# First feed forward block of an attention and feed forward kernel: order of steps from a list scheduler in place of a table

## The chip, the core and the metric

The kernel runs on one core of a Trainium2 chip. A core has TensorE (PE in the profile; its loads of the stationary operand are PEld), VectorE (DVE), ScalarE (ACT), GpSimd (POOL) and SyncE (SP, which issues DMAs). Each engine takes its instructions from a queue of its own, in program order, and waits at semaphores for what others produce. The metric is device time in microseconds. Three runs of the kernel before took 734.34, 735.73 and 742.5 us; the median is 735.73.

## What is computed

Attention with a learned bias over relative positions, then two feed forward blocks. Only the first of these is touched:

```python
def _moe_ref(x, w_in, w_out, a, b):      # x 1152 x 512, d_ff 2048
    h = x @ w_in
    h2 = h * h
    h3 = h2 * h
    P = a[0] + a[1] * h + a[2] * h2 + a[3] * h3
    Q = 1.0 + np.abs(b[0]) * np.abs(h) + np.abs(b[1]) * h2
    g = P / (Q + 1e-06)
    return (g @ w_out).astype(np.float32)
```

The second block is `maximum(0.01 * h, h)` between two products of the same sizes.

## The kernel before

Matrices are split in a high and a low part of a short float type, and a product is the sum of three: high by high, high by low, low by high.

The hidden width of 2048 is cut into NF = 16 slices of 128, called f. For each f there is a round of steps:

- `gemm1(f, kk)`, kk = 0 to 3 (PE, line 399): 9 matmuls each, 36 for one f, into one of two PSUM areas `ph`. An f can only start when `r_v(f - 2)` has read the area.
- the rational function, on tiles of 128 x 1152: `r_abs` (ACT, 435), `r_s1` (ACT, 439), `r_qa` (DVE, 443), `r_qq` (ACT, 446), `r_h2` (DVE, 449), `r_h3` (DVE, 452), `r_ln` (ACT, 456), `r_exp` (ACT, 459), `r_q1` (ACT, 464), `r_e` (POOL, 470; on DVE, 468, for f = 0, 1, 2, and then without `r_q1`), `r_v` (DVE, 473), `r_fin` (DVE, 476). `r_e` needs `r_exp` and `r_q1`; `r_v` needs `r_h3` and `r_exp`; `r_fin` needs `r_e` and `r_v`. Tiles rotate through 3 buffers (`s`, `qq`), 2 (`r`) and 1 (`ah`).
- `split_hi` (ACT, 489) and `split_lo` (POOL, 494; on DVE for f = 0, 1, 9) make the two parts `gh` and `gl` of the result. Both need `r_fin`.
- the weights for later f, a group t at a time: `w_load` (SP, 337), three `w_dve` steps that turn 64-bit floats into 32-bit (DVE, 356, 358, 360; operands `biasr` and `raw`, all in SBUF), `w_hi` (ACT, 370) and `w_lo` (POOL, 378). A group has two weight slices, the last ones have one and their steps are half as wide. `w_dve` of a group writes the one buffer `raw` that `w_lo` of the group before reads.

The second product runs over blocks of f (`BLOCKS = [1, 2, 2, 2, 3, 3, 3]`). For each block it makes 12 tiles of 128 x 384 (`g2_feat`; PE, line 976, 3 matmuls for each f of the block), and each tile is added to a sum in SBUF by DVE (line 984, 0.55 us; for the first block ACT copies it, 982). Tiles rotate through two PSUM buffers `py`.

What sets the order before is the table `PLAN1`: a list of (step, name) pairs. A loop counts s up, four s for one f, and at each s emits the instructions of the table in its order, each for the f that (s - step)/4 gives. Tiles of the second product are put in between by a credit that grows at an even rate; a block comes into the queue `G2_LAG[0]` = 12 steps after its last f. For the last f, all steps go in thirds of the columns. So each f repeats the same order on each engine:

```python
PLAN1 = [
    (4, "r_v"),
    (5, "w_lo", 0),
    (-3, "gemm1", 0),
```

`START` is a list of steps that are emitted ahead of the loop (the last steps of f = 0, `gemm1` of f = 1, four tiles of the first block); it stays. The second feed forward block has its own table, `PLAN2`, and follows.

Of the kernel before, what the change touches and what calls it, by code (L numbers as in the profile page):

```python
# [31 lines left out]
PLAN1 = [
    (4, "r_v"),
    (5, "w_lo", 0),
    (-3, "gemm1", 0),
    (-3, "gemm1", 1),
    (2, "r_h3"),
    (8, "split_hi"),
    (-2, "gemm1", 2),
    (2, "w_dve", 0),  # L40
    (3, "w_dve", 2),
    (-2, "gemm1", 3),
    (0, "r_qa"),
    (5, "w_hi", 1),
    (8, "split_lo", (1, 9)),
    (-1, "r_abs"),
    (0, "r_s1"),
    (3, "r_exp"),
    (5, "w_lo", 1),
    (1, "r_h2"),  # L50
    (4, "r_q1"),
    (1, "r_qq"),
    (2, "w_dve", 1),
    (4, "w_hi", 0),
    (2, "r_ln"),
    (7, "r_fin"),
    (4, "w_load"),
    (4, "r_e"),
]
# [211 lines left out]
def attn_bias_moe_kernel(  # L271
# [754 lines left out]
    w_ops = {x.__name__: x for x in (w_dve, w_hi, w_lo)}
    w_ops["w_load"] = lambda t: w_load(t + 1)
    for m, plan, g2_lag, fn, args in (
        ("1", PLAN1, G2_LAG[0], g2_feat, [(n, c) for n in range(KD) for c in range(3)]),
        ("2", PLAN2, G2_LAG[1], g2_tok, [(t,) for t in range(NT // 128)]),  # L1030
    ):
# [17 lines left out]
        for s in range(4 * (NF + 5)):
            ready = s - g2_lag  # L1050
            if m == "1" and (s == G2_FIRST or ready == 0):
                if s == G2_FIRST:
                    queue += [(0, a) for a in first]
                    rate = len(args) / 4
            elif ready % 4 == 0 and ready // 4 in block_end:
# [93 lines left out]
```

## Time and profile before

| | |
|---|---|
| runs | 734.34, 735.73, 742.5 us |
| profiled execution | 741.0 us, of which the span from first to last instruction 739.2 us |
| granted TensorE clock, mean of the span | 0.937 |
| PE, DVE, ACT, POOL busy | 615.1, 527.4, 391.7, 365.0 us |
| first feed forward block | about 273 to 535 us of the span |

A busy share is an average over the whole span; the stages differ. In the slices of the page PE is busy to 60 to 90% from 270 to 510 us, and to 100% behind that. Where an engine waits, the profile names what ended the wait.

### The profile page before, as it was taken

The page shows a single profiled execution, that of the slowest core. Times are in us where ns is not written, and L with a number is a line of the kernel's source. Part 1 is how long each engine was busy: PE and PEld are TensorE (multiplying, and loading weights), DVE is VectorE, ACT ScalarE, POOL GpSimd, SP SyncE. Part 2 cuts the span into 40 slices and gives each one's busy share as a digit, 9 for nine tenths or more (in the row PEclk, how much of TensorE's full clock was granted, in tenths as well). Part 3 has the DMA queues.
Part 4 walks back from the last instruction along what each step waited for, and adds up shares of the span by engine and source line. Part 5 has one row for each costly group of instructions (what it writes and reads, how often), then busy time and mean ns, then how long its engine had stood idle before and what let it go on. Part 6 is the DMA issues. An engine that isn't in the chain of part 4 may idle for free. (4 is left out here: it accounts for less than half of the span.)

```text
span 739.2 us, 11793 instructions
## 1 busy us (share of the span) xinstructions
PE 615.1 (83%) x4595; PEld 542.0 (73%) x4595; DVE 527.4 (71%) x837; ACT 391.7 (53%) x590; POOL 365.0 (49%) x270
## 2 busy tenths in 40 slices
PE   4566669988887867669797778977999999999998
PEld 2333458777776866668686778976999989999876
DVE  7999688888788488867577787675725664654463
ACT  5687367787686448664555556662325423323220
POOL 4676567787688212263544435545125535345240
PEclk9998789999899889779999899999999999999999
DMA  3999989999999611211111121001113313222013
GB/s 126 142 134 133 155 169 197 195 200 189 179 207 177 162 66 55 107 57 58 57 58 58 57 108 35 30 29 57 58 58 114 113 58 114 75 96 86 29 57 129
DMA packets 104359, 77.35 MB, mean 105 GB/s; under 512 B 86512, under 2 KB 86896, under 8 KB 104304
## 3 DMA queue, kind: packets, MB, share of 16 engines
q1 hardware_dynamic: 100704, 68.97, 41.3%
q10 hardware_dynamic: 3600, 7.64, 3.9%
q8 instruction: 36, 0.59, 0.4%
q14 instruction: 19, 0.16, 0.1%
HBM read 42.38 MB, written 2.36 MB: 61 GB/s over the span
## 5 line engine op out<-in xcount | busy, mean ns | idle before, releaser
L399 PE MATMUL ph<-bias,bias 128*128 128x384 f32 x1152 | 227.3, 353 | 24.2 <-DVE s L473 21.1
L399 PEld LDWEIGHTS ph<-bias,bias 128*128 128x128 f32 x1152 | 216.4, 201 | 31.5 <-issue 23.6
L824 POOL TENSOR_TENSOR hl<-ex,hl 128x512 f16<-128x512 f32 (+2 forms) x105 | 104.3, 1011 | 36.5 <-DVE hl L811 19.9
L494 POOL TENSOR_TENSOR gl<-s,gh 128x1152 fp32r<-128x1152 f32 (+1 forms) x31 | 77.8, 2513 | 89.0 <-ACT gh L489 89.0
L976 PE MATMUL py<-gh,wo 128*128 128x384 f32 x288 | 85.5, 355 | 27.6 <-DVE bias L984 27.6
L759 PE MATMUL ps<-kt,qz 128*128 128x288 f32 x432 | 84.0, 336 | 19.5 <-DVE mn L771 9.9
L759 PEld LDWEIGHTS ps<-kt,qz 128*128 128x128 f32 x432 | 67.1, 210 | 32.0 <-DVE mn L771 14.6
L378 POOL TENSOR_TENSOR bias<-raw,bias 128x512 fp32r<-128x512 f32 x37 | 48.5, 1314 | 73.2 <-ACT bias L370 66.9
L976 PEld LDWEIGHTS py<-gh,wo 128*128 128x128 f32 x288 | 55.4, 197 | 31.9 <-DVE bias L984 31.9
L1017 DVE TENSOR_TENSOR bias<-pz,bias 128x512 f32<-128x512 f32 x48 | 33.1, 689 | 60.0 <-PE pz L1009 59.8
L1009 PE MATMUL pz<-wo,gh 128*128 128x512 f32 (+1 forms) x240 | 74.4, 386 | 0.3 <-DVE bias L1017 0.3
L378 POOL TENSOR_TENSOR wo<-raw,wo 128x512 fp32r<-128x512 f32 x23 | 29.8, 1294 | 78.5 <-ACT wo L370 78.5
L685 POOL TENSOR_TENSOR t<-t,te 128x576 f32<-128x576 f32 x36 | 50.8, 1415 | 33.1 <-ACT t L681 15.1
L670 PEld LDWEIGHTS <-coef 128*32 128x32 f16 x1152 | 27.7, 104 | 52.6 <-issue 40.6
L787 ACT ACTIVATE ex<-pt,mn 128x576 f32<-128x576 f32 x72 | 55.3, 767 | 18.1 <-DVE mn L771 10.9
L489 ACT ACTIVATE gh<-s 128x1152 fp32r<-128x1152 f32 (+1 forms) x33 | 36.1, 1100 | 48.9 <-DVE s L476 41.2
L984 DVE TENSOR_TENSOR bias<-py,bias 128x384 f32<-128x384 f32 x72 | 39.0, 553 | 31.4 <-PE py L976 31.3
L356 DVE TENSOR_SCALAR raw<-biasr 128x1024 int32<-128x1024 int32 (+1 forms) x40 | 28.5, 712 | 40.5 <-POOL bias L378 19.2
L976 PE MATMUL py<-gl,wo 128*128 128x384 f32 x156 | 54.2, 347 | 0.0
L771 DVE CUSTOM_DVE_ANT_0 pt<-ps,bias 128x576 f32<-128x576 f32 x64 | 47.7, 747 | 7.6 <-PE ps L759 5.2
L1009 PEld LDWEIGHTS pz<-wo,gh 128*128 128x128 f32 x240 | 44.3, 188 | 8.1 <-DVE bias L1017 0.7
L1009 PE MATMUL pz<-wo,gl 128*128 128x512 f32 (+1 forms) x129 | 50.1, 389 | 0.0
(134 smaller groups left out, 1131.9 us busy)
## 6 DMA issues: line engine op xcount, KB each, us to landing
biasr<-in_moe_w_in SPq DMA_DIRECT2D x32, 512.0 KB, 4.3
biasr<-in_moe_w_out SPq DMA_DIRECT2D x32, 512.0 KB, 3.3
bias<-bb SPq DMA_DIRECT2D x32, 288.0 KB, 8.8
vl<-in_v ACTq DMA_DIRECT2D x8, 320.0 KB, 3.6
ql<-in_q ACTq DMA_DIRECT2D x8, 288.0 KB, 4.3
kl<-in_k ACTq DMA_DIRECT2D x8, 288.0 KB, 4.9
out<-bias SPq DMA_DIRECT2D x8, 256.0 KB, 2.0
biasr<-bb SPq DMA_DIRECT2D x8, 144.0 KB, 8.9
```

The lines of the kernel that those rows point to most:

```text
L378: G.tensor_tensor(lo_, raw[:, x], hi_.bitcast(F32), ALU.subtract)
L399: PE.matmul(ps[:, c, 0:CH], w[:, sl], x[kk][:, c * CH:(c + 1) * CH], start=(kk == 0 and n == 0), stop=(kk == KD - 1 and n == 2),)
L489: A.activation(part(gts[f][0], c), part(s1[f], c), AF.Copy)
L494: eng.tensor_tensor(part(gl, c), part(s1[f], c), part(gh, c).bitcast(F32), ALU.subtract)
L685: G.tensor_tensor(t1, t0, te[:, S - 16 * n:2 * S - 16 * n], ALU.mult)
L759: PE.matmul(ps[:, c, 0:288], lt[:, a], kts[i][:, b, 288 * c:288 * c + 288], start=(n == 0), stop=(n == 2),)
L771: V.tensor_tensor_reduce(out=c2(pt), in0=s_ps.pop((i, j))[:, :, 0:288], in1=c2(bsrc), op0=ALU.add, op1=ALU.min, scale=1.0, scalar=3.0e38, ...
L787: A.activation(et, pt, AF.Exp, bias=mn, scale=-1.0, accum_out=sums[i][:, col:col + 1],)
L824: engines[j in at].tensor_tensor(hl[:, xs, dst], e9[:, xs, src], hl[:, xs, src], ALU.subtract)
L976: PE.matmul(ps[:, 0:CH], w[:, sl], gts[f][x][:, cs], start=(f == f0 and m == 0), stop=(f == f0 + nf - 1 and m == 2),)
L984: V.tensor_tensor(dst, ps[:, 0:CH], dst, ALU.add)
L1009: PE.matmul(ps[:, half], gts[f][x][:, sl], w[:, half], start=(f == f0 and m == 0), stop=(f == f0 + nf - 1 and m == 2),)
```

## The change

The table `PLAN1` and the credit for the first block go. In their place `plan_first` lists every step of the block behind `START` as a task with its engine, a cost in us, whether it uses the port of SBUF that DVE and POOL share (`port`), and the steps that it waits for. `arrange` then begins the tasks one by one in a modelled time: it takes the engine that can begin first, and there, among the tasks that can begin within `SLACK` of the first, the one whose way to the end is longest, with a number for each kind of step added (`SHIFT`). A task with `port` also waits until the port is free. The tasks are emitted in the order in which they begin. `g2_feat` is cut in two, `g2_mm` (matmuls) and `g2_acc` (sum), so that the sum can be emitted later than its tile. `split_lo` of f = 1 and 9 is emitted for POOL. `r_e` and `r_q1` are as before (`E_DVE` stays, so f = 1 and 2 have `r_e` on DVE), though the planner reckons with POOL there (`E_DVE_1` is empty). The instructions are otherwise the same ones.

```diff
-PLAN1 = [
-    (4, "r_v"),
...
+COST = {
+    "gemm1": ("PE", 1.56, 0), "g2_mm": ("PE", 0.52, 0), "g2_acc": ("V", 0.56, 0), "g2_out": ("A", 0.55, 0),
...
+SLACK = 0.19
+
+
+def arrange(tasks, ends, free):
...
+    def longest(k):
+        if k not in way:
+            way[k] = tasks[k][3] + max((longest(u) for u in users[k]), default=0.0)
+        return way[k]
+
+    for k in reversed(tasks):
+        longest(k)
+    rank = {k: way[k] + SHIFT[k[0]] for k in tasks}
...
+    while todo:
+        best = {}
+        for k, r in ready.items():
+            eng, port = tasks[k][0], tasks[k][1]
+            t = max(free.get(eng, 0.0), r, free.get("port", 0.0) if port else 0.0)
+            best.setdefault(eng, []).append((t, k))
+        first = {e: min(t for t, k in xs) for e, xs in best.items()}
+        eng = min(first, key=first.get)
+        t, k = max(((t, k) for t, k in best[eng] if t <= first[eng] + SLACK), key=lambda x: rank[x[1]])
+        end = t + tasks[k][3]
+        free[eng] = end
+        if tasks[k][1]:
+            free["port"] = end
...
+    begun.sort(key=lambda x: x[0])
+    return [k for t, k in begun]
...
-    def g2_feat(bi, n, c):
+    py = {}
+
+    def g2_mm(bi, n, c):
...
+    def g2_acc(bi, n, c):
+        cs, ps = slice(c * CH, (c + 1) * CH), py.pop((bi, n, c))
...
+                add(("r_abs", *x), [last, ("r_qa", f - 1)], part)
+                add(("r_s1", *x), [last, ("split_lo", f - 3)], part)
+                add(("r_qa", *x), [("r_abs", *x), ("r_fin", f - 3)], part)
...
+            for k in plan_first(args, by_chunk):
...
+                elif k[0] == "split_lo":
+                    split_lo(k[1], (), *k[2:])
...
```

What it does to the queues, at two places. POOL before, in the middle of the block: one `r_e` (line 470), two `w_lo` (378) and one `split_lo` (494) for each f, in turn. The rows run from `r_e` of f = 10 to `split_lo` of f = 11; names end in the number of a buffer.

```order
L470 TENSOR_TENSOR qq<-qq,r_5211 128x1152
L378 TENSOR_TENSOR wo_4199<-raw,wo_4198 128x512
L378 TENSOR_TENSOR bias_74<-raw,bias_74 128x512
L494 TENSOR_TENSOR gl<-s_5143,gh 128x1152
L470 TENSOR_TENSOR qq<-qq,r_5309 128x1152
L378 TENSOR_TENSOR wo_4201<-raw,wo_4200 128x512
L378 TENSOR_TENSOR bias_74<-raw,bias_74 128x512
L494 TENSOR_TENSOR gl<-s_5241,gh 128x1152
```

POOL with the change, at f = 8 to 10 (line 503 is `r_e`, 411 `w_lo`, 527 `split_lo`):

```order
L503 TENSOR_TENSOR qq<-qq,r_4944 128x1152
L503 TENSOR_TENSOR qq<-qq,r_5086 128x1152
L411 TENSOR_TENSOR wo_4197<-raw,wo_4196 128x512
L411 TENSOR_TENSOR bias_74<-raw,bias_74 128x512
L527 TENSOR_TENSOR gl<-s_4934,gh 128x1152
L527 TENSOR_TENSOR gl<-s_5038,gh 128x1152
L411 TENSOR_TENSOR wo_4199<-raw,wo_4198 128x512
L411 TENSOR_TENSOR bias_74<-raw,bias_74 128x512
L503 TENSOR_TENSOR qq<-qq,r_5188 128x1152
```

`r_e` and `split_lo` of two f stand behind each other, with the `w_lo` between them. DVE before, one round from `w_dve` to the next `r_h3`, at f = 10 and 11 (356, 358 and 360 are `w_dve`, 984 a partial sum, 476 `r_fin`, 473 `r_v`, 443 `r_qa`, 494 the `split_lo` of f = 9 that is on DVE, 449 `r_h2`, 452 `r_h3`):

```order
L356 TENSOR_SCALAR raw<-biasr 128x1024
L358 SCALAR_TENSOR_TENSOR raw<-biasr,raw 128x1024
L984 TENSOR_TENSOR bias_73<-py,bias_73 128x384
L360 SCALAR_TENSOR_TENSOR raw<-biasr,raw 128x1024
L476 SCALAR_TENSOR_TENSOR s_5037<-qq,s_5037 128x1152
L984 TENSOR_TENSOR bias_73<-py,bias_73 128x384
L473 SCALAR_TENSOR_TENSOR s_5143<-ph,nab,r_5211 128x1152
L443 SCALAR_TENSOR_TENSOR qq<-ah,babs,ph 128x1152
L494 TENSOR_TENSOR gl<-s_5037,gh 128x1152
L984 TENSOR_TENSOR bias_73<-py,bias_73 128x384
L449 TENSOR_TENSOR s_5241<-ph,s_5241 128x1152
```

DVE with the change, from `r_fin` of f = 6 on (509 `r_fin`, 1023 a partial sum, 485 `r_h3`, 506 `r_v`, 482 `r_h2`, 476 `r_qa`, 389 the first `w_dve` step):

```order
L509 SCALAR_TENSOR_TENSOR s_4684<-qq,s_4684 128x1152
L509 SCALAR_TENSOR_TENSOR s_4818<-qq,s_4818 128x1152
L1023 TENSOR_TENSOR bias_73<-py,bias_73 128x384
L485 SCALAR_TENSOR_TENSOR ph<-s_4934,nab,ph 128x3x384
L1023 TENSOR_TENSOR bias_73<-py,bias_73 128x384 x2
L506 SCALAR_TENSOR_TENSOR s_4934<-ph,nab,r_4944 128x1152
L482 TENSOR_TENSOR s_5038<-ph,s_5038 128x1152
L1023 TENSOR_TENSOR bias_73<-py,bias_73 128x384 x2
L476 SCALAR_TENSOR_TENSOR qq<-ah,babs,ph 128x1152
L485 SCALAR_TENSOR_TENSOR ph<-s_5038,nab,ph 128x3x384
L389 TENSOR_SCALAR raw<-biasr 128x1024
```

`r_fin` of f = 6 and f = 7 now stand together, before `r_h3` and `r_v` of f = 8, and `r_h2`, `r_qa` and `r_h3` of f = 9 follow ahead of the next `w_dve`. On ACT, `r_s1`, `r_qq`, `r_ln` and `r_q1` of an f stand ahead of `split_hi` of the f two before.

## Rows read from the trace of the kernel before

**Rows 1.** Busy time by stretches: us, then PE, PEld, DVE, ACT, POOL, clock, DMA.

```profile
273.15:324.89 51.74, 37.69 (x181) 35.49 (x180) 41.81 (x35) 36.53 (x41) 14.77 (x9) 0.89 0.22 81
324.89:487.39 162.50, 133.64 (x690) 128.08 (x690) 119.22 (x130) 92.34 (x91) 74.52 (x38) 0.93 0.16 59
487.39:534.78 47.39, 38.91 (x199) 37.48 (x200) 32.36 (x62) 19.43 (x37) 20.46 (x14) 0.93 0.13 46
580.00:700.00 120.00, 120.00 (x609) 109.27 (x608) 66.42 (x77) 34.01 (x40) 53.22 (x30) 1.00 0.23 80
```

**Rows 2.** Groups by line and shape, 273.15 to 534.78: busy us, mean ns, idle before.

```profile
L984 DVE TENSOR_TENSOR bias<-py,bias 128x384 f32<-128x384 f32 x71 | 38.4, 553 | 30.9 <-PE py L976 30.8
L470 POOL TENSOR_TENSOR qq<-qq,r 128x1152 f32<-128x1152 f32 x12 | 32.2, 2682 | 28.9 <-ACT qq L464 18.2 <-DVE bias L984 10.7
L494 POOL TENSOR_TENSOR gl<-s,gh 128x1152 fp32r<-128x1152 f32 x12 | 31.9, 2657 | 80.4 <-ACT gh L489 80.4
...
L452 DVE SCALAR_TENSOR_TENSOR ph<-s,nab,ph 128x1152 f32<-128x1152 f32 x14 | 19.8, 1416 | 0.1
...
L476 DVE SCALAR_TENSOR_TENSOR s<-qq,s 128x1152 f32<-128x1152 f32 x14 | 18.9, 1351 | 0.0
```

**Rows 3.** Order of time, one round: start us, length us, engine, line, operation.

```profile
411.23 1.41 DVE L443 SCALAR_TENSOR_TENSOR qq<-ah,babs,ph 128x1152 f32<-128x1152 f32 x1
...
412.74 1.31 ACT L439 ACTIVATE s<-ph,nab 128x1152 f32<-128x1152 f32 x1 [2.02 <-DVE qq L443]
413.95 1.25 ACT L464 ACTIVATE qq<-qq,onep 128x1152 f32<-128x1152 f32 x1
...
415.34 2.69 POOL L470 TENSOR_TENSOR qq<-qq,r 128x1152 f32<-128x1152 f32 x1 [1.89 <-ACT qq L464]
...
419.21 1.31 POOL L378 TENSOR_TENSOR bias<-raw,bias 128x512 fp32r<-128x512 f32 x1
...
420.55 0.69 DVE L356 TENSOR_SCALAR raw<-biasr 128x1024 int32<-128x1024 int32 x1 [1.38 <-POOL bias L378]
...
421.28 1.23 DVE L358 SCALAR_TENSOR_TENSOR raw<-biasr,raw 128x1024 int32<-128x1024 int32 x1
...
422.90 1.21 DVE L360 SCALAR_TENSOR_TENSOR raw<-biasr,raw 128x1024 int32<-128x1024 int32 x1
...
424.03 1.35 DVE L476 SCALAR_TENSOR_TENSOR s<-qq,s 128x1152 f32<-128x1152 f32 x1
...
425.76 1.41 DVE L473 SCALAR_TENSOR_TENSOR s<-ph,nab,r 128x1152 f32<-128x1152 f32 x1
427.09 1.40 DVE L443 SCALAR_TENSOR_TENSOR qq<-ah,babs,ph 128x1152 f32<-128x1152 f32 x1
...
431.18 2.69 POOL L470 TENSOR_TENSOR qq<-qq,r 128x1152 f32<-128x1152 f32 x1 [10.65 <-DVE bias L984]
```

**Rows 4.** Chain that ended last: start us, us, what (with its count of matmuls).

```profile
463.44 1.57 PE py L976 x9
465.00 3.12 PE ph L399 x18
...
509.50 25.28 PE py L976 x135
```

**Rows 5.** Order of time on DVE: the block's first step, and `r_qa` of f = 5, 15.

```profile
270.88 0.69 DVE L356 TENSOR_SCALAR raw<-biasr 128x1024 int32<-128x1024 int32 x1
...
324.89 1.40 DVE L443 SCALAR_TENSOR_TENSOR qq<-ah,babs,ph 128x1152 f32<-128x1152 f32 x1
...
487.39 1.65 DVE L443 SCALAR_TENSOR_TENSOR qq<-ah,babs,ph 128x384 f32<-128x384 f32 x3
```

**Rows 6.** Order of time: a half-size `w_dve` step beside POOL, and one alone.

```profile
466.26 1.29 POOL L378 TENSOR_TENSOR bias<-raw,bias 128x512 fp32r<-128x512 f32 x1
466.84 1.00 DVE L356 TENSOR_SCALAR raw<-biasr 128x512 int32<-128x512 int32 x1
...
481.93 0.43 DVE L356 TENSOR_SCALAR raw<-biasr 128x512 int32<-128x512 int32 x1 [1.00 <-POOL bias L378]
```

**Rows 7.** DMA issues of the page: KB each, median us from issue to landing.

```profile
biasr<-in_moe_w_in SPq DMA_DIRECT2D x32, 512.0 KB, 4.3
biasr<-in_moe_w_out SPq DMA_DIRECT2D x32, 512.0 KB, 3.3
```

More of the change, by code (lines that the diff above doesn't have):

```diff
@@ L27 @@
 SIGN_FROM = 3
-G2_FIRST = 6
 O_LAG = (0, 1)
 O_STEP = (3, 0)
-G2_LAG = (12, 10)
-PLAN1 = [
-    (4, "r_v"),
[L34 to L59, printed above, removed]
+G2_LAG = 10
@@ new lines @@
+COST = {
[6 rows of a table added]
+}
+E_DVE_1 = ()
+SHIFT = {'g2_acc': 85.7, 'g2_mm': 40.9, 'g2_out': 8.3, 'gemm1': 162.0, 'r_abs': 97.9, 'r_e': -55.8, 'r_exp': 33.0, 'r_fin': -7.4, 'r_h2': 273.8, 'r_h3': -41.1, 'r_ln': -253.7, 'r_q1': 51.6, 'r_qa': -51.7, 'r_qq': 199.1, 'r_s1': -20.3, 'r_v': 10.2, 'split_hi': 262.3, 'split_lo': 61.1, 'w_dve0': 177.5, 'w_dve1': 15.3, 'w_dve2': 11.6, 'w_hi': 90.2, 'w_lo': 57.9, 'w_load': 106.7}
+SLACK = 0.19
+def arrange(tasks, ends, free):
+    way = {}
+    after = {k: [x for x in t[2] if x in tasks] for k, t in tasks.items()}
+    users = {k: [] for k in tasks}
+    for k, xs in after.items():
+        for x in xs:
+            users[x].append(k)
+    def longest(k):
[5 more added lines that the diff above has]
+    rank = {k: way[k] + SHIFT[k[0]] for k in tasks}
+    ends, free, todo, begun = dict(ends), dict(free), dict.fromkeys(tasks), []
+    ready = {k: max([ends.get(x, 0.0) for x in tasks[k][2]], default=0.0) for k in tasks if not after[k]}
+    missing = {k: len(after[k]) for k in tasks}
+    while todo:
[11 more added lines that the diff above has]
+            free["port"] = end
+        ends[k] = end
+        begun.append((t, k))
+        del todo[k], ready[k]
+        for u in users[k]:
+            missing[u] -= 1
+            if not missing[u]:
+                ready[u] = max(ends.get(x, 0.0) for x in tasks[u][2]) + 0.15
+    begun.sort(key=lambda x: x[0])
+    return [k for t, k in begun]
@@ L1023, in attn_bias_moe_kernel, with plan_first, add, parts @@
         for x in (r_abs, r_s1, r_qq, r_qa, r_h2, r_h3, r_ln, r_exp, r_q1, r_e, r_v, r_fin)
-        + (l_001, l_max, split_hi, split_lo)
+        + (l_001, l_max, g2_mm, g2_acc, w_hi, w_lo)
     }
+    ops["gemm1"] = early["gemm1"]
+    ops["split_hi"] = split_hi
+    ops["split_lo"] = split_lo
+    def plan_first(rest, by_chunk):
+        tasks = {}
+        def add(key, waits, part=1.0):
+            eng, cost, port = COST[key[0]]
+            if key[0] == "r_e" and key[1] in E_DVE_1:
+                eng, cost, port = "V", 1.41, 1
+            tasks[key] = (eng, port, list(waits), cost * part + 0.12 * (part < 1.0))
+        def parts(f):
+            return [(f, c) for c in range(3)] if f == NF - 1 else [(f,)]
+        units, held = [], {}
+        for bi, (f0, nf) in enumerate(blocks):
+            for n, c in (rest if bi == 0 else by_chunk if bi == len(blocks) - 1 else all_args):
+                units.append((bi, n, c))
+            for f in range(f0, f0 + nf):
+                held[f] = bi
+        u_of = {bi: [u for u in units if u[0] == bi] for bi in range(len(blocks))}
+        slots = {"i": len(wi_ring), "o": len(wo_ring)}
+        def w_tasks(t):
+            add(("w_load", t), [("w_dve2", t - 1)]) if t else None
+            pair = w_pair.get(t, ())
+            part = len(pair) / 2
+            add(("w_dve0", t), [("w_load", t)] + [(x, t - 1, y) for x in ("w_hi", "w_lo") for y in range(2)], part)
+            add(("w_dve1", t), [("w_dve0", t)], part)
+            add(("w_dve2", t), [("w_dve1", t)], part)
+            for x, (m, f) in enumerate(pair):
+                old = f + NF * (m[1] == "2") - slots[m[0]]
+                if m[0] == "i":
+                    used = [("gemm1", old, KD - 1)]
+                else:
+                    used = [("g2_mm", *u) for u in u_of[held[old]]] if old >= 0 else []
+                add(("w_hi", t, x), [("w_dve2", t)] + used)
+                add(("w_lo", t, x), [("w_hi", t, x)])
+                if m[1] == "1":
+                    made[m[0], f] = ("w_lo", t, x)
+        made = {}
+        for t in range(NF + 3):
+            w_tasks(t)
+        add(("w_load", NF + 3), [("w_dve2", NF + 2)])
+        for f in range(1, NF):
+            if f > 1:
+                for kk in range(KD):
+                    add(("gemm1", f, kk), [("gemm1", f, kk - 1) if kk else ("gemm1", f - 1, KD - 1)]
+                        + [made.get(("i", f))] + [("r_v", *x) for x in parts(f - 2)])
+            part = 1 / len(parts(f))
+            last = ("gemm1", f, KD - 1)
+            for x in parts(f):
+                c = x[1:]
+                add(("r_abs", *x), [last, ("r_qa", f - 1)], part)
+                add(("r_s1", *x), [last, ("split_lo", f - 3)], part)
+                add(("r_qa", *x), [("r_abs", *x), ("r_fin", f - 3)], part)
+                add(("r_qq", *x), [("r_qa", *x)], part)
+                add(("r_h2", *x), [("r_s1", *x)], part)
+                add(("r_ln", *x), [("r_qq", *x), ("r_v", f - 2), ("r_e", f - 2)], part)
+                add(("r_h3", *x), [("r_h2", *x), ("r_qa", *x)], part)
+                add(("r_exp", *x), [("r_ln", *x)], part)
+                if f not in E_DVE_1:
+                    add(("r_q1", *x), [("r_ln", *x)], part)
+                add(("r_v", *x), [("r_h3", *x), ("r_exp", *x)], part)
+                add(("r_e", *x), [("r_exp", *x), ("r_q1", *x)], part)
+                add(("r_fin", *x), [("r_v", *x), ("r_e", *x)], part)
+                gone = [("g2_mm", *u) for u in u_of.get(held.get(f - 2 * max(BLOCKS)), ())]
+                add(("split_hi", *x), [("r_fin", *x)] + gone, part)
+                add(("split_lo", *x), [("split_hi", *x)], part)
+        before = []
+        for u in units:
+            bi, n, c = u
+            f0, nf = blocks[bi]
+            fs = range(f0, f0 + nf)
+            waits = [("split_lo", *x) for f in fs for x in parts(f) if len(x) == 1 or x[1] == c]
+            acc = "g2_acc" if bi else "g2_out"
+            add(("g2_mm", *u), waits + [made.get(("o", f)) for f in fs] + before[-2:-1] + before[-3:-2], nf)
+            add((acc, *u), [("g2_mm", *u)])
+            before += [("g2_mm", *u), (acc, *u)]
+        return arrange(tasks, {("gemm1", 1, KD - 1): 6.0, ("w_load", 0): 2.0}, {"PE": 8.0, "A": 2.0, "G": 4.0, "V": 1.0})
@@ L1040, in attn_bias_moe_kernel @@
                 early[name](*a)
-            first = args
-            args = [(n, c) for n in range(KD) for c in range(3)]
+            for k in plan_first(args, by_chunk):
+                if k[0] == "w_load":
+                    w_load(*k[1:])
+                elif k[0].startswith("w_dve"):
+                    w_dve(k[1], int(k[0][5:]))
+                elif k[0] == "split_lo":
+                    split_lo(k[1], (), *k[2:])
+                elif k[0] == "g2_out":
+                    g2_acc(*k[1:])
+                else:
+                    ops[k[0]](*k[1:])
+            x_low()
+            continue
         else:
@@ L1050, in attn_bias_moe_kernel @@
             ready = s - g2_lag
[L1051 to L1055, printed above, removed]
+            if ready % 4 == 0 and ready // 4 in block_end:
                 bi = block_end[ready // 4]
-                queue += [(bi, a) for a in (by_chunk if m == "1" and bi == len(blocks) - 1 else args)]
+                queue += [(bi, a) for a in args]
                 rate = len(args) / (4 * blocks[min(bi + 1, len(blocks) - 1)][1])
```

15 lines of the change are left out of this document (8 added, 7 removed), and 5 rows, old and new, of the table COST.

## The prediction

> **What bounds the kernel now.** I read the busy time by stretches first, then the groups by line, then the order of time of one round, then the chain of waits. The first feed forward block runs from 273.15 us to 534.78 us, 261.6 us of a span of 739.2. In its long middle part, from `r_qa(5)` to `r_qa(15)`, no engine is full [rows 1]: PE is busy 133.6 of 162.5 us at a granted clock of 0.93, DVE 119.2, ACT 92.3, POOL 74.5. Behind it, in the second block, PE is busy all the time at a clock of 1.00. So this part is bound by an order, not by an engine, and the order is what the change replaces.
>
> The rows in order of time show which one [rows 3]. Read them as a ring, from `r_qa` at 411.23 to the next at 427.09: `r_qa` on DVE, then on ACT `r_s1` (which starts when `r_qa` ends) and `r_q1` behind it, then on POOL `r_e`, `w_lo`, `w_lo` (to 420.52), then on DVE the three `w_dve` steps, `r_fin` (424.03), a partial sum, `r_v`, and `r_qa` again. Each step starts where the one before ends, within 0.2 us. The ring takes 15.86 us and holds one f; the ten f from `r_qa(5)` at 324.89 to `r_qa(15)` at 487.39 [rows 5] take 162.5 us, 16.25 each. The 0.4 us above the ring (2.5%) are stray waits for PE and PSUM.
>
> **What one f costs at least.** PE: 36 matmuls of `gemm1` and 36 of the second product; 9 in a row take 1.57 us and 18 take 3.12 [rows 4], so 72 x 0.1735 = 12.5 us at full clock. DVE: five `r_` steps of 1.35 to 1.42 us (6.9 together), a group of three `w_dve` (0.69 + 1.23 + 1.21, 3.1), and 72/15 = 4.8 partial sums of 0.55 [rows 2, 3]; that is 12.7 by lengths, and about 12.0 because a row starts some 0.08 us before the last one ends (`r_v` 425.76, 1.41 long, `r_qa` 427.09). The third load is a pair: POOL's `r_e` 2.68, `split_lo` 2.66 and two `w_lo` of 1.3, and DVE's `w_dve` and `r_fin`, whose operands all lie in SBUF. Where such a DVE step met a POOL step, it stretched: a half-size first `w_dve` step at 466.84, beside a `w_lo` that ran to 467.55, took 1.00 us, and alone 0.43 [rows 6]. Taken as work that can only go in turn, the pair has 7.9 + 4.5 = 12.4 by lengths, about 12.1 with the overlaps. So all three loads are 12.0 to 12.5, against 16.25 now: up to 3.75 us per f can be had, not more.
>
> The Trainium skill has the rule for the pair (SBUF — State Buffer, Who interferes with whom): a DVE instruction with two SBUF inputs, or in a two-port mode, and a GpSimd instruction hold one port pair in turn, and the loser blocks for the whole instruction. The trace agrees in direction (1.00 against 0.43), though the wait there was a little shorter than the rest of the `w_lo`. By the rule the pair goes in turn as I take it; without it the ten f would be PE's 12.5 each, 8 us less in all than the 13.3 that I come to below. The rule also speaks against an order that stacks POOL work; that is the second rival.
>
> **The change, part by part.** It adds no work. Two `split_lo` (f = 1 and 9) go from DVE (1.35) to POOL (2.66), which has room now (busy 46% of the middle). Everything else is order. In the queues shown above, POOL's round of `split_lo`, `r_e`, `w_lo`, `w_lo` becomes runs of two: two `r_e`, two `w_lo`, two `split_lo`, two `w_lo`. On DVE, `r_fin` of two f stand nearly together, ahead of `r_h3` and `r_v` of the next one, and `r_h2`, `r_qa` of the f behind are already in the stretch in which POOL works. On ACT, `r_s1`, `r_ln` and `r_q1` of an f stand ahead of `split_hi` of the f before last. So `r_fin` no longer feeds `r_v`, `r_qa`, `r_s1`, `r_q1` and `r_e` of one ring: the 5.4 us from `r_v` (425.76) over `r_qa`, `r_s1` and `r_q1` to POOL's next `r_e` (431.18) [rows 3], in which neither port step nor POOL step ran but one `split_lo`, lie beside POOL's work. What is late next is the pair in turn, and PE. SP's loads move with the last `w_dve` step and have 9 us to land; the medians are 4.3 and 3.3 [rows 7].
>
> I followed the new queues by hand with these lengths, each instruction starting when its queue and its inputs allow. From `r_fin(8)` = 0: `r_fin(9)` to 3.0; POOL `split_lo` 8 and 9 to 8.3, two `w_lo` to 10.9, `r_e(10)` to 13.5, while DVE does `r_h3`, `r_v`, `r_h2`, `r_qa`, `r_h3` and five sums to 12.1; `w_dve` to 16.5; a sum; `r_fin(10)` to 18.3; POOL two `w_lo`, `split_lo(10)`, `r_e(11)` to 26.1, DVE `r_v`, `r_qa`, `r_h2`, `r_h3` and three sums to 25; `w_dve` to 29.1; POOL `r_e(12)`, two `w_lo` to 34.3, DVE `r_v`, `r_h2`, `r_qa` and sums to 34.5; a half-size `w_dve` to 36.25, then `r_fin(11)`. Three f in 36.25: 12.1 each, PE idle 1.5 us in them. The four f before, followed the same way, take 52.0, 13.0 each, since more sums stand between.
>
> *Start.* DVE from 270.88 to `r_qa(5)`: four `w_dve` groups and a half (14.1), four each of `r_qa`, `r_h2`, `r_h3`, `r_v` (21.4 by starts), two `r_e` on DVE (2.7), two `r_fin` (2.5): 40.7, and 4.7 of waits that I meet on the way (the first `r_abs` 1.8, `r_s1(3)` and `r_s1(4)` 2.4, POOL 0.5). That is 316.4 instead of 324.89 [rows 5]. *Middle.* By the rounds above `r_qa(15)` comes 128.6 us later, 12.9 per f. The same kind of ring gave 15.86 before, where 16.25 was measured; I put the same 2.5% and a little more on the start and the middle: 317.6, and 13.3 per f, 133 us instead of 162.5. *Tail.* At `r_qa(15)` PE still has 21 tiles of 9 matmuls. The last three thirds of `split_lo(15)` come, followed by hand, 12 to 20 us after it, before PE needs them, so PE sets the tail: 189 x 0.174 = 32.9; at the rate of the old tail, 25.28 us for 135 [rows 4], 35.4. I take 35.4, where 47.39 stand now.
>
> Sum: 7.3 + 29.5 + 12.0 = 48.8 us. The profiled execution took 741.0 (span 739.2 and 1.8 around it), so it would take 692.2. It lies 5.3 above the median of the runs, 735.73; against that the kernel takes **687 us**. Best end: PE's 12.5 per f, 316.4 at the start, 32.9 for the tail: 37.5 + 8.5 + 14.5 = 60.5, 675. If PE's matmuls stay at the 0.194 us that the middle shows (133.6 us for 690, at 0.93 of the clock), an f takes 13.9: 694.
>
> **Rivals.** *The sums wait for PE.* A partial sum stands in DVE's fixed queue and holds all behind it until its tile is done; PE has two tiles in PSUM and waits for the sum. Before, DVE lost 30.9 us in that way over 28 waits [rows 2], 2.05 per f. The new order has as many sums, in twos, and PE nearer to its limit. If the loss stays, on top of 12.5, an f takes 14.55 and the gain is 17.0 there, 4 at the start and 8 in the tail: 707. Against it: the sums stand behind tiles that my timeline has ready.
>
> *The pair of ports costs more (the other side).* The new queues let DVE's four port steps per f (three `w_dve`, `r_fin`) come up while POOL has its next instruction ready. If each loses its turn to one POOL step (7.98/4 = 2.0 us in the mean), an f takes 12.9 + 8.0 = 20.9, and the middle is 46.5 longer; start and tail give back 19: 763. It decides from 18.2 us per f on, that is 5.3 us lost per f. For it: 466.84 [rows 6]. Against it: `w_dve` and `w_lo` feed each other, so POOL has often nothing ready but one step. The skill's lock would work like this, since there the first to ask wins.
>
> *The ring stays.* If `r_qa` and `r_s1`, which go one after the other [rows 3], still tie two f together, the ten f take 158.6, 3.9 less, and a tail of 45 gives 2.4: 729. Against it: in the new queues `r_s1` stands ahead of POOL's run, so the two no longer close a ring.
>
> **How the numbers follow.** Forecast (675 to 700) 0.60, sums 0.26 (700 to 715), ring 0.07, ports 0.07. A measurement of this kernel tells about 1% from no change. Faster by over that: forecast and sums and a little of the ring, 0.88; within: the rest of the ring and a weak case of the ports, 0.06; slower 0.06. The range 675 to 714 leaves out the last two rivals and the edges.
>
> **What would show it.** `r_qa(5)` near 317, `r_qa(15)` near 450, end of the block's matmuls near 486; PE busy over 90% of the middle with a clock near 1.00; POOL's idle time ahead of `split_lo`, now the longest of all [rows 2], down by two thirds; `r_fin` at 1.35 us in the main, not stretched. The forecast is wrong if an f takes over 14 us: with idle time at the sums for PE, the first rival; with `w_dve` or `r_fin` rows of 2 us and more, the second.

## The result and the profile after

The changed kernel takes 688.17 us in the median of four runs (685.84 to 690.58); the kernel before, on the same chip, takes 735.04 (732.06 to 742.5). The ratio is 0.935, with an interval of 0.927 to 0.943. The forecast was 687.

The profiled execution took 687.9 us with a span of 686.1. Three things in it can be set against the span of 739.2 before. All that stands ahead of the block is 3.9 us shorter (the block starts at 269.25, where [rows 1] have 273.15); none of it was edited, and the profiled execution of before lay 5.3 above the median of its runs, so this part is a difference of executions. The block takes 212.6 us instead of 261.6: 49.0 less. Behind it stand 204.3 us, and 204.4 before. So the gain lies in the edited block, all of it.

Busy time by stretches, in the columns of [rows 1] (us, then PE, PEld, DVE, ACT, POOL, granted clock, DMA share, GB/s): from the block's start to `r_qa(5)`, to `r_qa(15)`, to the block's end, and a piece of the second block.

```profile
269.25:316.18 46.93, 34.53 (x170) 33.34 (x169) 39.12 (x34) 36.57 (x41) 22.01 (x11) 0.85 0.22 80
316.18:448.13 131.95, 126.64 (x711) 122.64 (x711) 126.82 (x135) 96.28 (x97) 85.55 (x42) 1.00 0.21 76
448.13:481.84 33.71, 33.39 (x190) 32.99 (x191) 30.99 (x57) 16.80 (x31) 14.67 (x12) 1.00 0.19 63
530.00:650.00 120.00, 120.00 (x608) 109.14 (x608) 66.70 (x79) 33.41 (x40) 50.67 (x29) 1.00 0.22 79
```

The ten f in the middle take 131.95 us where they took 162.50. PE and DVE are both busy for 96% of it, where PE had 82% and DVE 73% [rows 1]; the granted clock is 1.00, the 2.4 GHz level, where it was 0.93.

Groups by line and shape over the block, in the columns of [rows 2] (busy us, mean ns of one | idle time of the engine ahead of them, and what ended it):

```profile
L527 POOL TENSOR_TENSOR gl<-s,gh 128x1152 fp32r<-128x1152 f32 x14 | 39.2, 2809 | 28.0 <-ACT gh L522 27.5 <-DMA biasr<-in_moe_w_out 0.5
L1023 DVE TENSOR_TENSOR bias<-py,bias 128x384 f32<-128x384 f32 x71 | 38.2, 551 | 3.4 <-PE py L1011 3.2
L503 POOL TENSOR_TENSOR qq<-qq,r 128x1152 f32<-128x1152 f32 x12 | 34.5, 2879 | 13.5 <-ACT r L492 9.0 <-issue 3.3 <-PE ph L432 1.2
...
L482 DVE TENSOR_TENSOR s<-ph,s 128x1152 f32<-128x1152 f32 x14 | 18.9, 1352 | 6.6 <-ACT s L472 6.6
L509 DVE SCALAR_TENSOR_TENSOR s<-qq,s 128x1152 f32<-128x1152 f32 x14 | 18.7, 1350 | 0.0
...
L393 DVE SCALAR_TENSOR_TENSOR raw<-biasr,raw 128x1024 int32<-128x1024 int32 x12 | 17.0, 1421 | 0.4
...
L391 DVE SCALAR_TENSOR_TENSOR raw<-biasr,raw 128x1024 int32<-128x1024 int32 x11 | 13.5, 1225 | 0.3
L389 DVE TENSOR_SCALAR raw<-biasr 128x1024 int32<-128x1024 int32 x11 | 11.4, 1033 | 0.0
```

The two long idle groups of [rows 2] have shrunk: POOL's ahead of `split_lo` from 80.4 to 28.0 us, DVE's ahead of the partial sums from 30.9 to 3.4. `r_fin` (line 509) has its unstretched length. The first `w_dve` step (line 389) has not: 1.03 us in the mean, against 0.69 in [rows 3].

The order of time shows the runs of two (start us, length us, engine, line):

```profile
388.37 1.35 DVE L509 SCALAR_TENSOR_TENSOR s<-qq,s 128x1152 f32<-128x1152 f32 x1
389.76 0.56 DVE L1023 TENSOR_TENSOR bias<-py,bias 128x384 f32<-128x384 f32 x1
390.24 1.35 DVE L509 SCALAR_TENSOR_TENSOR s<-qq,s 128x1152 f32<-128x1152 f32 x1
391.42 5.33 POOL L527 TENSOR_TENSOR gl<-s,gh 128x1152 fp32r<-128x1152 f32 x2 [6.79 <-ACT gh L522]
...
426.85 2.62 DVE L509 SCALAR_TENSOR_TENSOR s<-qq,s 128x1152 f32<-128x1152 f32 x2
```

`r_fin(8)` and `r_fin(9)` stand together with one sum between them, the two `split_lo` follow as one run of 5.33 us, and `r_fin(11)` comes 38.48 us after `r_fin(8)`.

### The profile page after: what moved, and what is told of

Same layout as the page of the kernel before. It is cut to its first block, busy times and chain, and to the rows that moved or that the text cites. A ratio compares the mean times of both kernels' runs of the same rounds, so it can differ in the third digit from the quotient of the medians.

```text
span 686.1 us, 11789 instructions
## 1 busy us (share of the span) xinstructions
PE 596.4 (87%) x4595; PEld 527.3 (77%) x4595; DVE 531.4 (77%) x835; ACT 392.4 (57%) x590; POOL 377.4 (55%) x272
## 4 chain that ended last, share of the span: by engine, by line
PE 43%; DVE 26%; DMA 10%; ACT 5%; issue 4%; POOL 2%; ACTq 0%; DVEq 0%; SPq 0%; POOLq 0%
PE ph L432 19%; PE pz L1052 13%; PE py L1011 7%; DMA et<-hl 6%; DVE raw L393 2%; DVE raw L391 2%; DVE ph L485 2%; DVE bias L1023 2%; POOL hl L857 2%; DVE raw L389 2%; DVE s L506 2%; PE ps L792 2%; DMA bias<-bb 2%; DVE pt L804 2%; DVE s L482 1%
## 5 line engine op out<-in xcount | busy, mean ns | idle before, releaser
L432 PE MATMUL ph<-bias,bias 128*128 128x384 f32 x1152 | 216.5, 342 | 15.3 <-DVE s L506 12.6
L432 PEld LDWEIGHTS ph<-bias,bias 128*128 128x128 f32 x1152 | 207.2, 193 | 21.1 <-issue 11.5
L527 POOL TENSOR_TENSOR gl<-s,gh 128x1152 fp32r<-128x1152 f32 (+1 forms) x33 | 85.5, 2595 | 34.4 <-ACT gh L522 33.9
L1011 PE MATMUL py<-gh,wo 128*128 128x384 f32 x288 | 80.4, 339 | 3.7 <-DVE bias L1023 3.1
L1011 PEld LDWEIGHTS py<-gh,wo 128*128 128x128 f32 x288 | 52.6, 188 | 7.4 <-DVE bias L1023 5.5
L1011 PE MATMUL py<-gl,wo 128*128 128x384 f32 x156 | 52.2, 335 | 0.0
L403 ACT ACTIVATE wo<-raw 128x512 fp32r<-128x512 f32 x27 | 17.0, 629 | 57.1 <-DVE raw L393 57.1
L514 ACT ACTIVATE s<-ph 128x1152 f32<-128x1152 f32 x16 | 18.2, 1136 | 54.5 <-PE ph L432 43.3
L703 PE MATMUL psB<-mk,coef 128*32 128x512 f16 (+1 forms) x576 | 28.2, 317 | 23.7 <-DVE bb L723 23.6
```

Source lines behind the costliest of these rows:

```text
L432: PE.matmul(ps[:, c, 0:CH], w[:, sl], x[kk][:, c * CH:(c + 1) * CH], start=(kk == 0 and n == 0), stop=(kk == KD - 1 and n == 2),)
L703: PE.matmul(ps[32 * c:32 * c + 32, lo:hi], coef[:, int(c >= SIGN_FROM), j, part], masks[n][c][:, lo // 64:hi // 64], start=(part == 0), st ...
L1011: PE.matmul(ps[:, 0:CH], w[:, sl], gts[f][x][:, cs], start=(f == f0 and m == 0), stop=(f == f0 + nf - 1 and m == 2),)
```

## The experiments

"Of the gain" below means of the 6.5% that the change gives. Differences in us are differences of ratios times the time of the kernel before that was measured beside the run.

**Was it the ring?** In the kernel before, one row of the table is moved: ACT's `r_q1` one s (a quarter of a round) earlier, so that it no longer stands behind `r_s1` of the next f.

```diff
     (3, "r_exp"),
+    (3, "r_q1"),
...
-    (4, "r_q1"),
```

> The kernel before, with one row of its table moved: r_q1 of an f stands behind r_exp of that f, a quarter round earlier, so that on ACT it is ahead of split_hi and r_s1 and POOL's r_e no longer waits for r_s1 of the next f. Ring theory: the ring of 15.86 us opens, and the next one is r_e 2.69, two w_lo 2.6, w_dve with a sum 3.5, r_fin 1.35, split_hi 1.2, split_lo 2.65 = 14.1 us per f; over the twelve f with r_e on POOL some 15 to 21 us less, 714 to 720. Rival (the sums that wait for PE bind): the ring has no part in it, within 4 us of the kernel before.

It took 727.29 us, ratio 0.984 (0.978 to 0.990): 12 us gained, short of the 15 to 21 that the ring theory asked for and well clear of the 4 of its rival. One round of it in order of time:

```profile
401.54 2.65 POOL L494 TENSOR_TENSOR gl<-s,gh 128x1152 fp32r<-128x1152 f32 x1 [6.81 <-ACT gh L489]
...
404.13 2.69 POOL L470 TENSOR_TENSOR qq<-qq,r 128x1152 f32<-128x1152 f32 x1
...
408.02 1.31 POOL L378 TENSOR_TENSOR bias<-raw,bias 128x512 fp32r<-128x512 f32 x1
...
410.50 1.22 DVE L358 SCALAR_TENSOR_TENSOR raw<-biasr,raw 128x1024 int32<-128x1024 int32 x1
...
412.62 1.22 DVE L360 SCALAR_TENSOR_TENSOR raw<-biasr,raw 128x1024 int32<-128x1024 int32 x1
413.75 1.35 DVE L476 SCALAR_TENSOR_TENSOR s<-qq,s 128x1152 f32<-128x1152 f32 x1
...
415.13 1.16 ACT L489 ACTIVATE gh<-s 128x1152 fp32r<-128x1152 f32 x1 [0.61 <-DVE s L476]
```

`r_qa`, `r_s1` and `r_q1` are out of the ring of [rows 3], and the next ring shows: `split_lo`, `r_e`, `w_lo`, `w_lo` on POOL, `w_dve` on DVE (with 0.9 us at a sum between 411.72 and 412.62), `r_fin`, `split_hi`, and `split_lo` of the next f. (In the round shown that one is f = 9, whose `split_lo` is on DVE.) This round, between two `r_qa` (401.97 to 416.81), takes 14.84 us instead of 15.86. The rounds from f = 6 and from f = 8 take 14.07 and 14.10, the 14.1 that was expected of the next ring.

Two rounds keep their length. From f = 5 and from f = 7 a round takes 20.0 us, where the kernel before has 19.95 and 18.90. In them DVE stands at partial sums until PE has done the tile, 6.9 us in each here, 6.8 and 5.8 before. The longest such wait from f = 5, first in the kernel before, then in this one:

```profile
334.97 0.56 DVE L984 TENSOR_TENSOR bias<-py,bias 128x384 f32<-128x384 f32 x1 [4.00 <-PE py L976]
328.82 0.56 DVE L984 TENSOR_TENSOR bias<-py,bias 128x384 f32<-128x384 f32 x1 [4.09 <-PE py L976]
```

So the ten f take 154.9 us, 15.5 each, and in these two rounds the first rival, the sums, has a part. One row of the table breaks the ring that I had read; a fixed round has other waits just behind it.

**Two `split_lo` on POOL.** The kernel before, with `split_lo` of f = 1 and 9 on POOL.

```diff
-    (8, "split_lo", (1, 9)),
+    (8, "split_lo", ()),
```

> The kernel before, with split_lo of f = 1 and 9 on POOL instead of DVE, the one edit of the change that is not order. Both stand beside ACT's r_s1 in the ring and POOL has room: within 3 us of the kernel before. If where the work lies gave the gain and not the order, it would be several us faster.

Ratio 0.998 (0.994 to 1.002): no gain by itself, as expected.

**What of the list scheduler gives the gain?** First the numbers for each kind of step are taken away, so that the longest way to the end alone ranks the tasks.

```diff
-SHIFT = {'g2_acc': 85.7, 'g2_mm': 40.9, 'g2_out': 8.3, 'gemm1': 162.0,
...
+SHIFT = dict.fromkeys(COST, 0.0)
...
```

> The changed kernel with every number of SHIFT at zero: longest way to the end first, nothing else. If the rule itself makes the order, the middle stays at 13 to 14.5 us per f and the time is 690 to 708. If the fitted numbers make it, the order falls back to over 15 us per f and the time to above 715.

709.85 us, where the kernel before took 739.4 beside it: ratio 0.958 (0.952 to 0.965). Neither theory's numbers came: the time lies just above the first one's 708, and from `r_qa(5)` to `r_qa(15)` this kernel takes 149.7 us, 15.0 per f, between its 14.5 and the over 15 of the second (780 matmuls of PE fall into that stretch, 711 with the change). The plain rule gives 64% of the gain (4.16 of 6.52%), and the table of numbers the rest. Then the scheduler is told that no task uses the shared port.

```diff
-            eng, cost, port = COST[key[0]]
+            eng, cost, port = COST[key[0]][0], COST[key[0]][1], 0
```

> The changed kernel, its planner told that no task uses the port that DVE and POOL share. Port theory: w_dve and r_fin are put beside POOL's steps, and rows of w_dve, r_fin, r_e and split_lo stretch by 1 to 2.7 us several times per f; the middle goes to 14 us per f and more, 695 to 715. If the shared port is no matter, within 4 us of the changed kernel.

734.53 us, ratio 0.994 (0.991 to 0.998). 44.1 us worse than the changed kernel, and worse than both theories had it: nine tenths of the gain go. Groups of this kernel over its block:

```profile
L1023 DVE TENSOR_TENSOR bias<-py,bias 128x384 f32<-128x384 f32 x72 | 38.8, 550 | 11.7 <-PE py L1011 11.4
L509 DVE SCALAR_TENSOR_TENSOR s<-qq,s 128x1152 f32<-128x1152 f32 x14 | 38.1, 2720 | 0.5 <-POOL qq L503 0.2
...
L391 DVE SCALAR_TENSOR_TENSOR raw<-biasr,raw 128x1024 int32<-128x1024 int32 x12 | 24.1, 2007 | 0.3
```

`r_fin` takes 2.72 us in the mean instead of 1.35, and the second `w_dve` step 2.01 instead of 1.23: 19.2 and 9.4 us in which DVE counts as busy and stands. The busy time by stretches says the same for the ten f:

```profile
324.43:485.79 161.36, 131.30 (x682) 125.65 (x683) 147.84 (x133) 94.87 (x96) 85.86 (x39) 0.93 0.18 62
```

DVE is busy 147.8 us here and 126.8 with the change, at about the same number of instructions; the ten f take 161.4 us and 132.0. In order of time:

```profile
340.99 2.68 POOL L527 TENSOR_TENSOR gl<-s,gh 128x1152 fp32r<-128x1152 f32 x1
...
341.86 3.02 DVE L509 SCALAR_TENSOR_TENSOR s<-qq,s 128x1152 f32<-128x1152 f32 x1
...
346.16 3.12 POOL L527 TENSOR_TENSOR gl<-s,gh 128x1152 fp32r<-128x1152 f32 x1 [2.49 <-ACT gh L522]
346.78 3.58 DVE L391 SCALAR_TENSOR_TENSOR raw<-biasr,raw 128x1024 int32<-128x1024 int32 x1
```

An `r_fin` that began 0.87 us into a `split_lo` ended 1.21 us behind that one's end. So "order" is too short a name for what the change does: an order that overlaps everything it can, without knowing this pair, gives almost nothing here. One caution: the table of numbers was kept, and it may fit only the order that the port gives; the two stretched lines hold 28.6 of the 44.1 us. And one part of the new order was not run alone: the sums that can now stand later than their tiles.

**What bounds the changed kernel?** Extra work of one kind was put on each engine in turn, and on two of them in the kernel before too. The added instructions compute the same values once more (a doubled tile starts anew in PSUM).

```diff
+                if k[0] == "r_v":
+                    r_v(*k[1:])
```

> The changed kernel with r_v issued twice for each f (the second writes the same values): 20 us more of DVE work that does not touch the shared port. DVE is busy 96% of the middle, so nearly all of it should show: 15 to 20 us more, 703 to 708. If the sums waiting for PE bound it, DVE would have room: under 8.

```diff
...
-        for f in range(f0, f0 + nf):
+        for f in twice * list(range(f0, f0 + nf)):
...
+                elif k[0] == "g2_mm" and k[2] == 0:
+                    g2_mm(*k[1:], twice=2)
```

> The changed kernel with the matmuls of the tiles n = 0 of the second product issued twice (the second run overwrites the first): 138 matmuls, 24 us more of PE work, 9 of it in the tail where PE alone sets the pace. PE is busy 96% of the middle at full clock: 18 to 24 us more, 706 to 712. If DVE alone binds the middle: about 9 to 12.

```diff
+                if k[0] == "w_lo" and k[2] == 0:
+                    w_lo(*k[1:])
```

> The changed kernel with the first w_lo of each group issued twice (same values): 22 us more of POOL work, which has to go in turn with w_dve and r_fin. POOL is busy 65% of the middle. Port theory: DVE's port steps wait for it, 8 to 18 us more. If POOL and DVE go side by side: under 4.

```diff
+                if k[0] == "r_abs":
+                    r_abs(*k[1:])
```

> The changed kernel with r_abs issued twice for each f (same values): 17 us more of ACT work. ACT is busy 73% of the middle and its steps have slack except at r_qa and r_h2, which wait for r_abs and r_s1: 2 to 8 us more. If ACT is on the path all along: 15 and more.

In the kernel before, `r_v` twice, and the same tiles twice:

> The kernel before with r_v issued twice for each f: 20 us more of DVE work. r_v is a link of the ring, so by the ring theory all of it shows, 18 to 21 us more, although DVE is busy only 73% of the middle. If no ring binds and DVE has room: under 8.

> The kernel before with the matmuls of the tiles n = 0 of the second product issued twice: 24 us more of PE work, some 9 of it in the tail where PE sets the pace. Ring theory: PE's idle time in the middle takes the rest, 7 to 13 us more. If the sums that wait for PE bind (rival), each later tile holds DVE: 18 us and more.

| added to | work added, us | changed kernel, us more | kernel before, us more |
|---|---|---|---|
| DVE | 20 | 16.9 (ratio 0.958, 0.954 to 0.961) | 19.0 (1.026, 1.016 to 1.035) |
| PE | 24 | 19.3 (0.961, 0.957 to 0.966) | 3.2 (1.004, 1.000 to 1.009) |
| POOL | 22 | 21.2 (0.964, 0.960 to 0.967) | not run |
| ACT | 17 | 15.7 (0.956, 0.950 to 0.962) | not run |

The row for PE shows what has changed: 24 us of matmuls cost 3 us before (7 to 13 were expected), because PE had idle time to take them, and 19 with the new order. A part of the 21 us hidden before may be quicker matmuls and not idle time filled: the granted clock of the whole run was 0.947 with them and 0.935 without, each the median of the runs. In the changed kernel with the added matmuls the sums wait again, 26.0 us of DVE's time ahead of them instead of 3.4:

```profile
L1023 DVE TENSOR_TENSOR bias<-py,bias 128x384 f32<-128x384 f32 x72 | 38.9, 551 | 26.0 <-PE py L1011 25.9
```

DVE cost nearly its full length in both, once as a full engine, once as a member of the ring. POOL and ACT were a surprise. POOL's 22 us were expected to cost 8 to 18 since it is busy for 65% of the middle. Its second `w_lo` makes the port steps on DVE longer:

```profile
L393 DVE SCALAR_TENSOR_TENSOR raw<-biasr,raw 128x1024 int32<-128x1024 int32 x12 | 19.5, 1623 | 0.4
L391 DVE SCALAR_TENSOR_TENSOR raw<-biasr,raw 128x1024 int32<-128x1024 int32 x12 | 19.4, 1616 | 0.4
...
L389 DVE TENSOR_SCALAR raw<-biasr 128x1024 int32<-128x1024 int32 x12 | 16.4, 1363 | 0.0
```

For 12 groups that is 4.0 us more in line 389, 4.7 in line 391 and 2.4 in line 393 than by the means of the changed kernel (1.03, 1.23 and 1.42): 11 of the 21.2 us, on an engine that is nearly full. DVE also waits 4.6 us more at sums for PE (7.8 against 3.2 over the block), in a middle whose granted clock was 0.95; what lowered the clock stays open. ACT, busy for 73% of the middle, was expected to hide its 17 us but for 2 to 8; it hid 1.3. The groups of that kernel show the place:

```profile
L1023 DVE TENSOR_TENSOR bias<-py,bias 128x384 f32<-128x384 f32 x68 | 36.5, 549 | 6.4 <-PE py L1011 6.0
...
L476 DVE SCALAR_TENSOR_TENSOR qq<-ah,babs,ph 128x1152 f32<-128x1152 f32 x14 | 19.7, 1407 | 8.6 <-ACT ah L468 7.3 <-ACT s L472 1.2
```

DVE waits 7.3 us at `r_qa` for the doubled `r_abs`, where the changed kernel waits 2.3, and some 4 us more at sums. It also waits 2.3 us more at `r_v`, 2.2 at `r_h2`, 1.0 at `r_qa` for `r_s1` and 0.8 for a load. Together that is 15 us more of DVE waiting, about the whole of the 15.7. A fixed order made for a length of 1.22 has no give for 2.4 at that place, however idle ACT is in the mean.

So the table does not single out one engine: work added to any of the four costs 80 to 96% of its length. That PE and DVE are the full ones rests on their busy shares of 96%; what the table shows is that this order leaves little room anywhere.

**Can the scheduler's knowledge be mended?** The changed kernel's start has waits that the scheduler does not know of (next section). Two kernels tell it more: that `r_s1` and `r_qa` of one f go in turn, and that `r_e` of f = 1 and 2 runs on DVE.

```diff
             t = max(free.get(eng, 0.0), r, free.get("port", 0.0) if port else 0.0)
+            if k[0] in ("r_s1", "r_qa"):
+                t = max(t, free.get(("ph", *k[1:]), 0.0))
...
+        if k[0] in ("r_s1", "r_qa"):
+            free["ph", *k[1:]] = end + 0.15
```

> The changed kernel, with one thing more that the scheduler knows: r_s1 and r_qa of one f read the same PSUM tile and are run in turn, as the trace of the changed kernel shows (r_s1 starts when r_qa ends), so the scheduler too holds the second until the first ends. Theory: the missing tie costs the waits of DVE for r_s1 in the start (four of about 1.4 us at f = 1 to 4), so r_qa(5) comes 1 to 4 us earlier (43 to 46 us behind the block's start instead of 46.9), the middle stays near 13.2 us per f, and the kernel takes 684 to 689. Rival: the scheduler's table of ranks fits the order that it gave without this tie, and those waits only fill time in which DVE has nothing else; then a new order loses elsewhere, r_qa(5) stays at 47 or later and the kernel takes 690 to 705.

```diff
-E_DVE_1 = ()
+E_DVE_1 = (1, 2)
```

> The changed kernel, with the scheduler told that r_e of f = 1 and 2 runs on DVE for 1.41 us (E_DVE_1 = (1, 2)), as it does on the chip, and that r_q1 of these two isn't issued; it had reckoned both on POOL at 2.69 us. Theory: the start is what these two touch, and an order made with the right engine has r_qa(5) 1 to 3 us earlier: 685 to 688. Rival, as for the other kernel: the ranks fit the old order, or POOL and the port have room in the start (busy 22 of 47 us), so nothing is gained: 688 to 700.

Both went the way of the rivals, and beyond their ranges, which ended at 705 and 700: 710.81 us (ratio 0.963, 0.957 to 0.968) and 711.53 (0.965, 0.959 to 0.970), 20.5 and 21.9 us behind the changed kernel. The stretches to `r_qa(5)`, to `r_qa(15)` and to the block's end, first with the tie:

```profile
275.24:344.76 69.52, 53.93 (x266) 51.82 (x266) 59.14 (x49) 41.05 (x46) 30.39 (x15) 0.87 0.20 68
344.76:465.66 120.90, 106.53 (x587) 102.78 (x586) 107.27 (x112) 86.79 (x85) 73.27 (x35) 0.97 0.21 71
465.66:507.20 41.54, 39.02 (x222) 37.95 (x221) 35.47 (x66) 20.80 (x37) 19.23 (x13) 1.00 0.19 63
```

and with `r_e` of f = 1 and 2 on DVE:

```profile
267.05:317.48 50.43, 37.41 (x183) 36.21 (x182) 43.49 (x35) 38.96 (x44) 21.18 (x11) 0.87 0.27 94
317.48:455.36 137.88, 124.00 (x670) 119.05 (x670) 121.00 (x126) 89.38 (x88) 82.98 (x39) 0.97 0.18 62
455.36:502.35 46.99, 41.75 (x220) 40.37 (x219) 36.85 (x64) 19.89 (x36) 17.56 (x12) 0.93 0.14 46
```

With the tie the start is 22.6 us longer, the ten f 11.1 shorter and the tail 7.8 longer; with `r_e` the three are 3.5, 5.9 and 13.3 longer. In the first, one group of `w_dve`, nine sums, two `r_fin` and an `r_h2` moved ahead of `r_qa(5)`, so that a part of the 22.6 us is work that the middle no longer has, and port steps met again. These rows of it show the pair best:

```profile
317.41 1.28 POOL L415 TENSOR_TENSOR wo<-raw,wo 128x512 fp32r<-128x512 f32 x1
317.50 2.41 DVE L513 SCALAR_TENSOR_TENSOR s<-qq,s 128x1152 f32<-128x1152 f32 x1
...
318.65 2.41 POOL L415 TENSOR_TENSOR bias<-raw,bias 128x512 fp32r<-128x512 f32 x1
...
326.87 2.65 POOL L507 TENSOR_TENSOR qq<-qq,r 128x1152 f32<-128x1152 f32 x1 [3.00 <-ACT r L496]
327.07 3.54 DVE L395 SCALAR_TENSOR_TENSOR raw<-biasr,raw 128x1024 int32<-128x1024 int32 x1
```

So a truer model did not give a better order. The likely reason is that the 24 numbers of `SHIFT` suit the one order that the old model gave; without them the rule lands at 709.85, in the same place as these two. That is an argument, not shown: a table fitted to the truer model was not run.

## Why the prediction was right, and where it was off

*Bound by an order.* Right. Moving one row of the old table gained 12 us without touching any work, and of 24 us added to PE the kernel before hid 21. The reading of the ring's remainder was wrong, though: the 0.4 us per f above 15.86 were not stray waits. The rounds from f = 5 and f = 7 took 19.95 and 18.90 us, with 6.8 and 5.8 us of DVE's waits at sums for PE, and the last one took 13.53.

*The middle.* Forecast 13.3 us per f, measured 13.2 (131.95 for ten). The bounds by load hold: PE busy 12.7 per f and DVE 12.7. The rounds followed by hand: `r_fin(4)` (336.51) to `r_fin(8)` (388.37) 51.86 against 52.0, `r_fin(8)` to `r_fin(11)` 38.48 against 36.25. The allowance of 0.4 per f that I took over from the old ring was about the right size (131.95 against 128.6 by hand is 0.3), and its content was another one; that it fitted is luck. DVE's port steps are 6 us longer over the block than alone: 11 first steps at 1.03 instead of 0.69, and 12 third ones (line 393) at 1.42 instead of 1.21 [rows 3]. The hand count had a part of that, as waits of DVE until `r_e` ends. It did not have the third step that makes up the 2.2 us by which the second of these rounds is longer:

```profile
415.59 3.16 POOL L503 TENSOR_TENSOR qq<-qq,r 128x1152 f32<-128x1152 f32 x1 [1.19 <-PE ph L432]
416.26 3.58 DVE L393 SCALAR_TENSOR_TENSOR raw<-biasr,raw 128x1024 int32<-128x1024 int32 x1
```

*The start.* This term was mis-sized: 7.3 us forecast, 4.8 measured (46.93 us from the block's start to `r_qa(5)`, 51.74 before). The step that failed is the list of waits "that I meet on the way". I had `r_h2` wait for `r_s1` at f = 3 and 4 only, 2.4 us; it waits in all four of f = 1 to 4. DVE's waits in the start (us in total, times, longest):

```profile
DVE s L482 <- ACT s L472: 5.6, 4, 1.4
DVE qq L476 <- ACT ah L468: 1.8, 1, 1.8
```

That is 5.6 us instead of 2.4; the wait for the first `r_abs` is the 1.8 that I had. The 1.2 us that I had put on top of the hand count of the start took up a part of the 3.2. `r_qa` and `r_s1` read the same PSUM tile, and each of the four `r_s1` starts within 0.1 us of the end of its `r_qa`. I used that tie in the ring of the kernel before; in the new queues `r_h2` is DVE's next step behind `r_qa` in all four, so that DVE has nothing to put there.

*The tail.* 12.0 forecast, 13.7 measured (33.71 against 47.39). PE sets it, as said (33.39 of 33.71 busy), and it runs at 1.00 of the clock. So the hand count at the full rate, 32.9, was the better estimate; the rate of the old tail, which I took, belonged to a stretch with a mean clock of 0.93 [rows 1].

The three errors, 2.5 too much and 1.1 and 1.7 too little, cancel: 48.8 forecast for the block, 49.0 measured. So part of the closeness of 687 to 688.17 is luck; each term alone was good to 3 us.

*The first rival, sums that wait for PE.* It asked for the 30.9 us of [rows 2] to stay; 3.4 are left. It was no empty rival: the two long rounds of the kernel before stood at sums, and the price was real: where PE is given more work, 26.0 us come back.

*The second rival, the pair of ports.* Its mechanism is real and its price was overdrawn. An order that does not know the pair loses 2.9 us per f (161.4 against 132.0), where I had put 8.0; that is enough to undo nine tenths of the change, not enough to make it slower. I gave it 0.07 on the ground that POOL often has nothing else ready. The better ground stood in the diff: the scheduler holds a task with `port` until the port is free. The Trainium skill (SBUF — State Buffer, Who interferes with whom) says that the first to ask has the pair for the whole instruction and the other blocks. The rows agree: the step from 327.07 ends 1.09 us after the `r_e` beside it, the `r_fin` from 317.50 ends 1.22 after the `w_lo`, and the next `w_lo` ends 1.15 after that `r_fin`, each 0.13 us less than its own length alone.

*The third rival, the ring stays.* It fell: ten f in 131.95, not 158.6.

*Signs.* The clock in the middle at 1.00, PE over 90% (96%), POOL's idle time ahead of `split_lo` down by two thirds (80.4 to 28.0, 65%) and `r_fin` at 1.35 all came as written. Set 3.9 us later, on the time axis of before, `r_qa(5)`, `r_qa(15)` and the end of the block came at 320.1, 452.0 and 485.7, where 317, 450 and 486 were written. `split_lo` of f = 1 and 9 on POOL cost nothing, as said.

## What to carry to other kernels

When a repeated stretch has no full engine, follow one round until it closes and ask what the next ring would be: moving one row gained 12 us here and met the next ring at once, while an order that takes all chains together came within 6% of PE's load (13.2 against 12.5 us per f). A static order has to hold every resource that two queues share, an SBUF port as well as an engine; such a loss shows as longer instructions, not as idle time, so compare mean lengths by line with the lengths alone. After a model or a rank table is edited, time the order anew, since a truer fact in the model cost 20 us here.

## What the runs showed of the hardware

A step of 1.22 us on DVE took up to 3.58 beside a 3 us step on POOL, and POOL's steps lose likewise (with the tie known to the scheduler, a `w_lo` of 1.28 took 2.41 behind an `r_fin`). I had expected DVE to lose now and then; in the order that ignores the pair, `r_fin` lost half of its time in the mean (2.72 for 1.35). The granted clock of the middle is 1.00 in the changed kernel, where PE runs on with hardly a gap; it is 0.93 in the kernel before and in the one without the port, where PE stands between tiles. At 0.93 a matmul took 0.194 us in the mean of the middle (133.64 for 690 in [rows 1]), and 0.178 at 1.00 (126.64 for 711). By these two means PE's work in the ten f is some 11 us shorter (an estimate, 711 times 0.016); that stands inside the 30.6 gained there and isn't added to them.
